# Transposes of keys, queries and last tokens moved behind attention-value products in a fused attention and expert kernel

## The chip, the cores and the metric

The kernel runs on one core of one Trainium2 chip. The time is the device time of one execution, in microseconds (us). The engines are TensorE (PE, with its weight loads as PEld), VectorE (DVE), ScalarE (ACT), GpSimd (POOL) and SyncE (SP, which here issues DMAs only).

## The reference

Attention with a relative-position bias, and behind it a mixture of experts that is routed by a hash of the token id:

```python
scores = scale * q @ k^T                    # 8 batches, 8 heads, 576 tokens, head size 64
scores = scores + bias_table[bucket(|i - j|)]    # one bias per head and distance bucket
attn = softmax(scores)
x = (attn @ v) laid out as 4608 tokens x 512
expert = token_ids * 2654435761 mod 8
out[token] = relu(x[token] @ w1[expert]) @ w2[expert]    # 512 -> 1024 -> 512
```

## The kernel before, in words

**Stages.** The attention stage runs up to about 222 us, writes each token's row with a scatter into a table in HBM that is sorted by expert, and the expert stage (line 802 on) then reads that table expert by expert. The change lies in the attention stage.

**Tiles of the attention.** Two heads make a pair; `pairs` lists 32 of them, four (m = 0 to 3) per batch b. Each pair has five groups g. Groups 0 to 3 are 128 keys each against 512 of the 576 queries; group 4 holds the rest, that is the last 64 tokens of the sequence, as queries and as keys. For a group, `products` multiplies keys and queries into one of three PSUM slots `ps`, `add_bias` adds the bias on TensorE, and `scores` has ScalarE write the exponentials to `att`. A third slot lets `add_bias` of the next group start early.

**The order.** It is written out by hand (lines 744 to 763): each engine works through its instructions in program order. A turn of the loop takes two groups and issues, on TensorE, the score products, the bias, then what `early` holds, then what `behind` holds for the first and for the second group, then the bias of the group that follows. `behind` advances a stream of attention-value (AV) products by nine per group. The stream runs one to two pairs behind the scores: pair p starts at group 2 of pair p+1. Its 45 steps are 27 for three output tiles in the PSUM bank aux0 and 18 for two in the bank aux1 (`px` in `av_steps`, line 511). At the end of each part VectorE takes a reciprocal (`rcp`, line 546) and multiplies into `x_all` (line 547), which empties the bank. As a pair has five groups, even pairs have groups 2 and 3 in one turn, odd pairs groups 3 and 4.

**What the change moves.**
- `transpose_qk` (line 370): eight TensorE transposes of the cast keys and queries of a pair into `pqk`, which has the bank aux1, and two VectorE copies to `kt` and `qt`. `early` issues it for pair n+2 at group 3 of pair n.
- `cast_rest` (line 246): two VectorE casts of the last tokens' queries and keys of the next batch (`qrh`, `krh`), in `behind` at (m, g) = (1, 3).
- `transpose_rest` (line 388): four transposes of these into `pr`, which has the bank aux0, and three VectorE copies to `kzr` and `qtr`; in `early` at (2, 0).
- `cast_vrest` (line 256): two POOL casts of the last tokens' values, in `pair_start` at m = 2, between `cast_qk` and the scatters.
- `load_rest` (line 199): eight DMAs on SP for the last tokens of a batch, in `pair_start` of the batch before (m = 0). Its tiles `qr`, `kr`, `vr` have one buffer each.

**Other work in the way.** `pair_start` also issues loads, the cast of `qh` and `kh` for three pairs ahead on POOL (two buffers each, so the cast waits for the transposes of two pairs before), and from pair 12 on two scatters per pair (`dispatch`, line 561, POOL; four in the last pairs). At pair 4 `route_load` has SP load the token ids into `te`; from pair 6 on `behind` issues one step of `route` per group, first on VectorE (`te`, `ef`, `oh`), then two ranking matmuls into `rps` (line 309).

Of the kernel before, what the change touches and what calls it, by code (L numbers as in the profile page):

```python
# [11 lines left out]
F32 = mybir.dt.float32  # L12
# [19 lines left out]
def kernel(  # L32
# [13 lines left out]
    B, H, S, D = q.shape  # L46
# [6 lines left out]
    P = 128  # L53
    NPAIR = H // 2
# [21 lines left out]
    for dl in range(3):  # L76
        for y in range(GN):
            r = 2 * y - MAXD + dl - 1
# [71 lines left out]
    with tc.tile_pool(name="at", bufs=1) as at, tc.tile_pool(  # L150
        name="atp", bufs=1, space=bass.MemoryType.PSUM
    ) as atp:

        def aux(i, shape, dtype, name):
            return atp.tile(shape, dtype, name=name, tag=f"aux{i}", bufs=1,
                            space=bass.MemoryType.PSUM)
# [24 lines left out]
        qr, kr, vr = {}, {}, {}  # L181

        def load(j, which="qkv", eng=None, h0=0, h1=4):
            for key, dst, src in (("q", qf, q), ("k", kf, k), ("v", vf, v)):
                if key not in which:
                    continue
                if j not in dst:
                    dst[j] = at.tile([P, 4, NT, 2 * D], F32, name=key + "f",
                                     bufs=3)
                for T in range(NT):  # L190
                    (eng or nc.sync).dma_start(  # L191
                        out=dst[j][:, h0:h1, T, :],
                        in_=bass.AP(
                            src.tensor, (4 * j + h0) * S * D + 2 * P * D * T,
                            [[2 * D, P], [S * D, h1 - h0], [1, 2 * D]],
                        ),
                    )

        def load_rest(b, which="qkv", eng=None):
            for key, dst, src in (("q", qr, q), ("k", kr, k)):  # L200
                if key not in which:
                    continue
                dst[b] = at.tile([P, 2, 2 * D], F32, name=key + "r", bufs=1)
                for hh in range(2):
                    (eng or nc.sync).dma_start(
                        out=dst[b][:, hh, :],
                        in_=bass.AP(
                            src.tensor, ((b * H + hh) * S + NB4) * D,
                            [[2 * D, RU], [2 * S * D, NPAIR], [1, 2 * D]],
                        ),  # L210
                    )
            if "v" in which:
                vr[b] = at.tile([P, NPAIR, D], F32, name="vr", bufs=1)
                for hh in range(2):
                    for c in range(2):
                        r0 = D * hh + RU * c
                        (eng or nc.sync).dma_start(
                            out=vr[b][r0 : r0 + RU, :, :],
                            in_=bass.AP(
                                v.tensor, ((b * H + hh) * S + NB4 + c) * D,  # L220
                                [[2 * D, RU], [2 * S * D, NPAIR], [1, D]],
                            ),
                        )
# [146 lines left out]
        def transpose_qk(n, eng=None):  # L370
            pqk = aux(1, [P, 2, KT * P], F16, "pqk")
            for i, src in enumerate((kh, qh)):
                for t in range(KT):
                    T, c = t // 2, t % 2
                    o = P * t if i == 0 else NT * P * c + P * T
                    nc.tensor.transpose(  # L376
                        out=pqk[:, i, o : o + P],
                        in_=src[n][:, t, :, :].rearrange("p h d -> p (h d)"),
                        identity=ident[:, :],
                    )  # L380
            kt = at.tile([P, KT * P], F16, name="kt", bufs=3)
            nc.vector.tensor_copy(out=kt[:, :], in_=pqk[:, 0, :])  # L382
            kts[n] = kt
            qt = at.tile([P, KT * P], F16, name="qt", bufs=3)
            nc.vector.tensor_copy(out=qt[:, :], in_=pqk[:, 1, :])
            qts[n] = qt

        def transpose_rest(b):
            pr = aux(0, [P, 2, 2, P], F16, "pr")
            for i, key in enumerate("kq"):  # L390
                for c in range(2):
                    nc.tensor.transpose(
                        out=pr[:, i, c, :],
                        in_=rh[b, key][:, c, :, :].rearrange(
                            "p h d -> p (h d)"
                        ),
                        identity=ident[:, :],
                    )
            for hh in range(2):
                nc.vector.tensor_copy(  # L400
                    out=kzr[b % 2][D * hh : D * hh + D, :,
                                   D * hh : D * hh + D].rearrange(
                        "p m (c u) -> p c m u", c=2
                    ),
                    in_=pr[D * hh : D * hh + D, 0, :, :].rearrange(
                        "p c (u m) -> p c m u", m=NPAIR
                    ),
                )
            nc.vector.tensor_copy(
                out=qtr[b % 2][:, :, :].rearrange(  # L410
                    "p m (c u) -> p c m u", c=2
                ),
                in_=pr[:, 1, :, :].rearrange(
                    "p c (u m) -> p c m u", m=NPAIR
                ),
            )
# [157 lines left out]
        def advance(it, count):  # L574
            for _ in range(count):
                if next(it, "end") == "end":
                    return
# [18 lines left out]
        nc.scalar.dma_start(out=idents[:, :, :], in_=I128_d.ap())  # L596
        load(0, "q", None, 0, 2)
        load_rest(0, "kq", nc.scalar)

        cast_qk(0, nc.vector, nc.vector)  # L600
# [63 lines left out]
        nc.sync.dma_start(out=msk[:, :], in_=MSK_d.ap())  # L664
        nc.sync.dma_start(out=cnt[:, :], in_=CNT_d.ap())
        nc.sync.dma_start(out=tok[:, :], in_=TOK_d.ap())
        load(2, "qk")

        FILLS = 10

        def fill_table(i):
            rows = NSLOT // FILLS
            nc.sync.dma_start(
                out=xperm_d.ap()[rows * i : rows * (i + 1), :].rearrange(
                    "(p r) d -> p (r d)", p=P
                ),
                in_=zx[:, :, :].rearrange("p r d -> p (r d)"),
            )

        NP = len(pairs)  # L680
# [12 lines left out]

        def pair_start(n):
            b, m = pairs[n]
            if b + 1 < B and m == 0:
                load_rest(b + 1)
            if n % 2 == 0 and n + 6 < NP:
                load(n // 2 + 3, "qk")
            if n % 2 == 0 and n + 4 < NP:  # L700
                load(n // 2 + 2, "v")
            if n == 4:
                route_load()
            if 2 <= n < 2 + FILLS:
                fill_table(n - 2)
            if n + 3 < NP:
                cast_qk(n + 3)
            if b + 1 < B and m == 2:
                cast_vrest(b + 1)
            if n >= 6 and pairs[n - 2][1] == 0:  # L710
                waiting.extend((pairs[n - 6][0], t) for t in range(NIT))
            if n >= 12:
                for _ in range(2 if n < NP - 2 else 4):
                    if waiting:
                        dispatch(*waiting.pop(0))
            if n >= 22 and n % 2 == 0 and n < 30:
                (load_w2 if n % 4 == 0 else load_w1)((n - 22) // 4)

        def behind(n, g):
            G = NIT * n + g  # L720
            b, m = pairs[n]
            if 6 <= n < 12:
                next(routing, None)
            if G >= NIT + 2:
                advance(av, 9)
            if g == 2 and n + 1 < NP:
                cast_v(n + 1)
            if (m, g) == (1, 3) and b + 1 < B:
                cast_rest(b + 1, nc.vector)

        def early(n, g):
            b, m = pairs[n]
            if (n, g) in ((0, 1), (1, 0)):
                transpose_qk(n + 1)
            if g == 3 and 0 < n < NP - 2:
                transpose_qk(n + 2)
            if (m, g) == (2, 0) and b + 1 < B:
                transpose_rest(b + 1)
            if (n, g) == (1, 0):
                rest_rest(0)  # L740
            if (m, g) == (3, 3) and b + 1 < B:
                rest_rest(b + 1)
# [25 lines left out]
    with tc.tile_pool(name="mo", bufs=1) as mo, tc.tile_pool(  # L768
        name="mop", bufs=1, space=bass.MemoryType.PSUM
# [83 lines left out]
    with tc.If(over > 0):  # L853
        with tc.tile_pool(name="fb", bufs=1) as fb, tc.tile_pool(
            name="fbp", bufs=1, space=bass.MemoryType.PSUM
# [126 lines left out]
```

## Time and profile before

| what | us |
|---|---|
| median of 3 runs | 396.09 (395.26 to 398.11) |
| the profiled execution | 397.42 |
| its span, first to last instruction | 395.6 |
| TensorE busy | 337.3 (85%) |
| ScalarE busy | 202.5 (51%) |
| GpSimd busy | 160.7 (41%) |
| VectorE busy | 133.2 (34%) |

Times in the rows are counted from the first instruction of the profiled execution. A matmul's end is modelled and matmuls overlap, so TensorE's pace is read from the starts. In brackets stands the idle time of the engine ahead of an instruction, and what ended it.

### The profile page before, as it was taken

What the parts mean: (1) busy time and instruction counts of PE and PEld (TensorE: products, weight loads), DVE (VectorE), ACT (ScalarE), POOL (GpSimd) and SP (SyncE); (2) the same over time, 40 slices, a digit from 0 to 9 for tenths busy, and PEclk for the clock granted to TensorE, in tenths of its full rate; (3) what the DMA queues carried; (4) which work ended last, traced back from release to release, by engine and by line L of the source; (5) the groups of instructions that cost most, each with busy time, mean ns of one, the idle gap of its engine ahead of it and who ended that gap; (6) DMA issues with size and microseconds to landing.
All of it is one profiled execution on the core that took longest, in us unless ns stands there. A gap on an engine that the chain in (4) does not pass through costs nothing.

```text
span 395.6 us, 9129 instructions
## 1 busy us (share of the span) xinstructions
PE 337.3 (85%) x3796; PEld 207.1 (52%) x3796; DVE 133.2 (34%) x322; ACT 202.5 (51%) x235; POOL 160.7 (41%) x229
## 2 busy tenths in 40 slices
PE   2667994999988889799998429999999999999990
PEld 1225662566555555465664316574756565665640
DVE  2204353554453433535422210405132322323120
ACT  1345881798778867788896204150504142332410
POOL 6125241142756656764743300334251515141231
PEclk9968997799999999999999958999999999999997
DMA  5998978999879487399871160799999999994221
GB/s 151 246 278 220 302 177 195 252 261 280 239 203 284 116 225 225 72 246 213 160 128 49 42 210 11 157 174 186 218 234 180 268 154 261 164 261 100 92 82 53
DMA packets 93491, 72.85 MB, mean 184 GB/s; under 512 B 14167, under 2 KB 84599, under 8 KB 93440
## 3 DMA queue, kind: packets, MB, share of 16 engines
q1 hardware_dynamic: 73616, 40.13, 37.9%
q0 software_dynamic: 17664, 30.96, 37.0%
q10 hardware_dynamic: 2160, 1.09, 1.0%
q8 instruction: 32, 0.52, 0.5%
q14 instruction: 19, 0.16, 0.1%
HBM read 69.47 MB, written 21.03 MB: 229 GB/s over the span
## 4 chain that ended last, share of the span: by engine, by line
PE 75%; DMA 8%; DVE 5%; SPq 4%; issue 2%; ACT 2%; POOL 1%; POOLq 0%; ACTq 0%; DVEq 0%
PE hps L812 18%; PE ops L830 17%; PE ps L441 11%; PE px L537 11%; PE ps L464 9%; PE pqk L376 4%; PE xps L791 3%; DVE x_all L547 2%; DMA qr<-in_q_dram 2%; SPq L191 2%; PE ps L498 2%; ACT att L506 2%; SPq L274 2%; DMA btb<-t_f 1%; DMA vf<-in_v_dram 1%
## 5 line engine op out<-in xcount | busy, mean ns | idle before, releaser
L506 ACT ACTIVATE att<-ps 128x1024 f16<-128x1024 f32 x160 | 153.4, 1026 | 53.1 <-PE ps L464 27.9
L818 ACT ACTIVATE h<-hps 128x640 f16<-128x640 f32 x64 | 45.1, 704 | 112.5 <-PE hps L812 112.2
L441 PE MATMUL ps<-btb,idents 128*128 128x384 f16 (+1 forms) x384 | 79.8, 294 | 3.5 <-DMA btb<-t_f 3.5
L812 PE MATMUL hps<-xpt,w1t 128*128 128x320 f16 x512 | 72.8, 303 | 0.0
L830 PE MATMUL ops<-w2t,h 128*128 128x512 f16 x320 | 72.7, 379 | 0.0
L838 POOL DMA_INDIRECT out_dram<-ok,xpn x40 | 39.2, 981 | 57.4 <-DVE ok L837 50.5
L812 PEld LDWEIGHTS <-w1t 128*128 128x128 f16 x512 | 50.8, 99 | 21.4
L537 PEld LDWEIGHTS <-att 128*128 128x128 f16 x1408 | 56.6, 99 | 7.2 <-issue 1.4
L537 PE MATMUL px<-va,att 128*128 128x65 f16 x1280 | 58.1, 195 | 0.9 <-issue 0.4
L830 PEld LDWEIGHTS <-h 128*128 128x128 f16 x320 | 30.7, 98 | 33.5
L562 POOL DMA_INDIRECT t_xperm<-x_all,ds x40 | 39.5, 987 | 19.0 <-DVE rcp L546 9.5
L464 PE MATMUL ps<-qt,kt 64*128 64x512 f16 x256 | 45.1, 401 | 1.5 <-ACT att L506 0.8
L441 PEld LDWEIGHTS <-idents 128*128 128x128 f16 x464 | 29.0, 99 | 30.9 <-issue 29.5
L837 DVE COPY ok<-ops 128x512 f32<-128x512 f32 x40 | 27.7, 692 | 46.9 <-PE ops L830 46.9
L795 DVE COPY xpt<-xps 128x640 f16<-128x640 f16 x32 | 15.0, 489 | 74.4 <-PE xps L791 73.4
L229 POOL CAST qh<-qf 128x512 f16<-128x512 f32 x31 | 19.1, 617 | 45.6 <-PE pqk L376 33.0
L237 POOL CAST va<-vf 128x512 f16<-128x512 f32 x32 | 19.8, 619 | 40.3 <-PE px L537 30.3
L546 DVE RECIPROCAL rcp<-px 128x6 f32<-128x6 f32 x64 | 11.9, 186 | 61.6 <-PE px L537 47.3
L547 DVE TENSOR_TENSOR x_all<-px,rcp 128x384 f16<-128x384 f32 x64 | 31.4, 491 | 2.2
L382 DVE COPY kt<-pqk 128x512 f16<-128x512 f16 x32 | 13.6, 425 | 51.4 <-PE pqk L376 49.2
L464 PEld LDWEIGHTS <-kt 64*128 64x128 f16 x512 | 14.0, 95 | 30.9 <-issue 27.8
L133 POOL DMA_DIRECT2D w1t<-in_moe_w_dram x8 | 6.5, 816 | 52.1 <-PE xps L791 52.1
(71 smaller groups left out, 243.8 us busy)
## 6 DMA issues: line engine op xcount, KB each, us to landing
w1t<-in_moe_w_dram POOLq DMA_DIRECT2D x8, 1024.0 KB
w2t<-in_moe_w_dram POOLq DMA_DIRECT2D x8, 1024.0 KB
qf<-in_q_dram SPq DMA_DIRECT2D x30, 256.0 KB
kf<-in_k_dram SPq DMA_DIRECT2D x30, 256.0 KB
vf<-in_v_dram SPq DMA_DIRECT2D x30, 256.0 KB
t_xperm<-zx SPq DMA_DIRECT2D x10, 514.0 KB
xpn<-t_xperm SPq DMA_DIRECT2D x8, 642.5 KB
vr<-in_v_dram SPq DMA_DIRECT2D x32, 32.0 KB
```

The source lines that it names most:

```text
L237: nc.gpsimd.tensor_copy(out=va[n % 3][:, :, :D], in_=vf[n // 2][:, 2 * (n % 2) : 2 * (n % 2) + 2].rearrange("p h t (c d) -> p (h t c) d", ...
L441: nc.tensor.matmul(out=out, lhsT=idents[:, which, :], rhs=rhs, start=start, stop=True, skip_group_check=True,)
L464: nc.tensor.matmul(out=ps[:, hh, o : o + rhs.shape[1]], lhsT=lhsT, rhs=rhs, start=not biased and (g < KT or t == 0), stop=True, skip_group ...
L506: nc.scalar.activation(out=att[:, g, :, :], in_=ps[:, :, :], func=AF.Exp, bias=0.0, scale=scale,)
L537: nc.tensor.matmul(out=po, lhsT=lhsT, rhs=rhs, start=(i == 0), stop=(i == len(todo) - 1), skip_group_check=True,)
L547: nc.vector.tensor_tensor(out=x_all[:, b, its[0] : its[0] + ni, :DM].rearrange("p t (m h d) -> p t m h d", h=2, m=NPAIR)[:, :, m, :, :], i ...
L562: sc_in = nc.gpsimd.indirect_dma_start(out=xperm_d.ap()[:, :], out_offset=bass.IndirectOffsetOnAxis(ap=ds2[:, B * t + b : B * t + b + 1], ...
L812: nc.tensor.matmul(out=hps[:, nr, :NR], lhsT=w1h[:, kt, ts(ft, P)], rhs=xt[e][:, kt, ts(nr, NR)], start=(kt == 0), stop=(kt == NPT - 1),)
L818: nc.scalar.activation(out=h1[:, ft, :].rearrange("p (r n) -> p r n", r=NRC), in_=hps[:, :, :NR], func=AF.Relu, bias=0.0, scale=1.0,)
L830: nc.tensor.matmul(out=ops[:, :], lhsT=h1[:, ft, ts(kc, P)], rhs=w2h[:, ft, :], start=(ft == 0), stop=(ft == NFT - 1),)
L837: nc.vector.tensor_copy(out=ok[:, :], in_=ops[:, :])
L838: so = nc.gpsimd.indirect_dma_start(out=out[:, :], out_offset=bass.IndirectOffsetOnAxis(ap=xn[e][:, kc, DM:XW].bitcast(I32), axis=0), in_= ...
```

## The change

`transpose_qk` at group 3 moves from `early` to `behind`, after the nine AV products of that group. `transpose_rest` moves there too, and from (2, 0) to (3, 0). `cast_rest` moves from (1, 3) to (2, 2), `cast_vrest` from m = 2 to m = 3. The last tokens' tiles get two buffers. The last tokens of batch 1 are loaded in the setup, ahead of the keys and queries of pairs 4 and 5, and no longer at pair 0.

```diff
-                dst[b] = at.tile([P, 2, 2 * D], F32, name=key + "r", bufs=1)
+                dst[b] = at.tile([P, 2, 2 * D], F32, name=key + "r", bufs=2)
...
-                vr[b] = at.tile([P, NPAIR, D], F32, name="vr", bufs=1)
+                vr[b] = at.tile([P, NPAIR, D], F32, name="vr", bufs=2)
...
         nc.sync.dma_start(out=tok[:, :], in_=TOK_d.ap())
+        load_rest(1)
         load(2, "qk")
...
-            if b + 1 < B and m == 0:
+            if 0 < b < B - 1 and m == 0:
                 load_rest(b + 1)
...
-            if b + 1 < B and m == 2:
+            if b + 1 < B and m == 3:
                 cast_vrest(b + 1)
...
             if G >= NIT + 2:
                 advance(av, 9)
+            if g == 3 and 0 < n < NP - 2:
+                transpose_qk(n + 2)
+            if (m, g) == (3, 0) and b + 1 < B:
+                transpose_rest(b + 1)
             if g == 2 and n + 1 < NP:
                 cast_v(n + 1)
-            if (m, g) == (1, 3) and b + 1 < B:
+            if (m, g) == (2, 2) and b + 1 < B:
                 cast_rest(b + 1, nc.vector)
 
         def early(n, g):
             b, m = pairs[n]
             if (n, g) in ((0, 1), (1, 0)):
                 transpose_qk(n + 1)
-            if g == 3 and 0 < n < NP - 2:
-                transpose_qk(n + 2)
-            if (m, g) == (2, 0) and b + 1 < B:
-                transpose_rest(b + 1)
             if (n, g) == (1, 0):
                 rest_rest(0)
```

## Rows read from the trace of the kernel before

**Rows 1.** Waits of TensorE: us in total, times, longest us.
```profile
PE pqk L376 <- DVE x_all L547: 8.5, 6, 4.3
PE pr L392 <- DVE x_all L547: 6.3, 7, 2.1
PE ps L464 <- ACT att L506: 2.4, 6, 0.8
```

**Rows 2.** Busy time by stretch: PE, PEld, DVE, ACT, POOL, PEclk, DMA, GB/s.
```profile
85.50:108.70 23.20, 22.08 (x354) 13.65 (x353) 10.85 (x30) 18.93 (x21) 12.21 (x19) 1.00 0.94 244
108.70:206.00 97.30, 88.10 (x1417) 55.36 (x1417) 42.81 (x117) 78.84 (x87) 60.38 (x86) 1.00 0.79 188
```

**Rows 3.** Timeline (start us, us, instructions) around one batch's last tokens.
```profile
87.83 0.75 DVE L249 CAST qrh<-qr 128x256 f16<-128x256 f32 x1
88.50 0.48 DVE L249 CAST krh<-kr 128x256 f16<-128x256 f32 x1
...
89.11 0.56 DVE L547 TENSOR_TENSOR x_all<-px,rcp 128x384 f16<-128x384 f32 x1
...
89.73 0.28 PE L392 MATMUL pr<-idents,krh 128*128 128x128 f16 x2 [0.69 <-DVE x_all L547]
```

**Rows 4.** Timeline around three pairs of scatters.
```profile
125.51 0.97 POOL L562 DMA_INDIRECT t_xperm<-x_all,ds  x1 [0.30 <-issue]
...
127.03 0.18 DVE L546 RECIPROCAL rcp<-px 128x4 f32<-128x4 f32 x1 [2.53 <-PE ps L441]
...
127.82 0.38 PE L376 MATMUL pqk<-idents,kh 128*128 128x128 f16 x4 [0.96 <-DVE x_all L547]
...
128.26 0.71 PE L537 MATMUL px<-va,att 128*128 128x65 f16 x18
...
131.16 0.97 POOL L562 DMA_INDIRECT t_xperm<-x_all,ds  x1 [0.30 <-issue]
...
132.67 5.62 ACT L506 ACTIVATE att<-ps 128x1024 f16<-128x1024 f32 x6 [1.10 <-PE px L537]
...
134.37 0.39 PE L376 MATMUL pqk<-idents,kh 128*128 128x128 f16 x4
...
138.72 0.97 POOL L562 DMA_INDIRECT t_xperm<-x_all,ds  x1 [0.30 <-issue]
...
141.01 0.38 PE L376 MATMUL pqk<-idents,kh 128*128 128x128 f16 x4 [1.14 <-DVE x_all L547]
```

**Rows 5.** Timeline around the first routing steps.
```profile
55.28 6.73 SPq L274 DMA_DIRECT2D te<-in_moe_token_ids_dram  x6
...
63.85 0.18 DVE L286 TENSOR_SCALAR te<-te 128x40 int32<-128x40 int32 x1 [3.78 <-DMA te<-in_moe_token_ids_dram]
...
64.97 0.59 PE L376 MATMUL pqk<-idents,kh 128*128 128x128 f16 x4 [4.34 <-DVE x_all L547]
...
66.69 0.87 DVE L299 TENSOR_TENSOR oh<-ef,msk 128x320 f16<-128x320 f32 x1
...
67.71 0.43 PE L309 MATMUL rps<-oh,cnt 128*128 128x320 f16 x1 [1.24 <-DVE oh L299]
...
70.02 1.02 ACT L506 ACTIVATE att<-ps 128x1024 f16<-128x1024 f32 x1 [8.06 <-PE ps L464]
```

**Rows 6.** Busy time of two stretches with a lower granted clock (columns as in rows 2).
```profile
30.00:40.00 10.00, 7.88 (x106) 5.14 (x102) 4.79 (x13) 5.74 (x6) 5.54 (x10) 0.83 0.81 221
60.00:75.00 15.00, 9.43 (x98) 5.75 (x96) 5.41 (x17) 5.47 (x6) 1.60 (x3) 0.66 0.96 251
```

**Rows 7.** Timeline of a turn with groups 4 and 0.
```profile
83.08 0.43 PE L537 MATMUL px<-va,att 128*128 128x65 f16 x9
83.36 0.49 PE L441 MATMUL ps<-btb,idents 128*128 128x384 f16 x2
83.52 0.56 DVE L547 TENSOR_TENSOR x_all<-px,rcp 128x384 f16<-128x384 f32 x1
```

**Rows 8.** Timeline of SP's queue around the early loads.
```profile
25.41 0.98 SPq L191 DMA_DIRECT2D qf<-in_q_dram  x2
...
33.05 0.98 SPq L191 DMA_DIRECT2D qf<-in_q_dram  x2
```

## The prediction

> **What bounds the kernel now.** I read the times first, then the waits of TensorE, the busy time by stretch, and last the timeline around the waits. The profiled execution took 397.42 us, 1.33 us over the median 396.09 (span 395.6). All sums are made against 397.42, and the 1.33 is taken off at the end. The change touches the attention stage alone, up to about 222 us; the expert stage behind it stays as it is.
>
> In the list of TensorE's waits the reader is to see that ScalarE holds TensorE for 2.4 us only, while the two transposes of this change wait for VectorE's `x_all` multiply: 8.5 us for `pqk` in 6 waits and 6.3 us for `pr` in 7 [rows 1]. The multiply empties the PSUM bank (aux1 for `pqk`, aux0 for `pr`) that the transposes want. In the windows, one batch of four pairs takes 23.2 us from 85.5 on. Once token scatters run twice per pair, the 97.3 us from 108.7 to 206 hold four batches, 24.3 us each: TensorE is idle for 97.3 - 88.1 = 9.2 us of them and ScalarE for 18.5 [rows 2]. So TensorE bounds the stage, with ScalarE close behind.
>
> The timeline shows three causes.
> - Last tokens: the casts `qrh` (0.75) and `krh` (0.48), 1.23 us together, stand on VectorE ahead of the reciprocal and the multiply at 89.11, and `pr` starts at 89.73 after 0.69 us of idle time [rows 3].
> - Scatters: TensorE goes on issuing, but what waits for it is released late, about 1.5 us after the start of the second scatter of a pair: scatter 125.51, reciprocal 127.03; 131.16 and ACT 132.67. I counted eleven such pairs between 106 and 193 us; two are shown. The `pqk` transposes then wait for the late multiply, 0.96 us at 127.82 and 1.14 at 141.01 [rows 4].
> - The token ids: SP issues the `te` loads in the 6.73 us from 55.28, VectorE's first routing step starts at 63.85, and everything behind it on VectorE, so also `pqk`, waits, 4.34 us. ScalarE stands still for 8.06 us until 70.02 [rows 5]. The granted clock of 60 to 75 us is 0.66, which is 10.2 us at half (1.2 GHz) and the rest at full (2.4 GHz); from 30 to 40 us it is 0.83, 3.4 us at half [rows 6].
>
> **Part 1: `transpose_qk` behind the products.** No instruction is added: eight transposes take 128.26 - 127.82 = 0.44 us in either place [rows 4]. For an even pair, (n,2) and (n,3) share a loop turn, so they now stand behind eighteen AV products (0.71 us with the tail, about 0.5 of issue); for an odd pair behind nine (0.28 us from 83.08 to the next work of TensorE at 83.36) [rows 4, 7]. AV products of that turn write aux0, which is free, so the even pairs' waits, 0.96 and 1.14 us in the rows, lose 0.5 us. But the casts of the next `qh` and `kh` on POOL wait for the transposes (both tiles have two buffers), and the scatters stand behind these casts on POOL. The scatters so start 0.28 us later behind an odd pair, and the release with them. Net 0.5 - 0.28, between 0.2 and 0.3, taken as 0.28, for each of five waits (the list has six, one of them the 4.34 of the token ids [rows 1, 5]): 5 x 0.28 = 1.4 us gained. Bounds: 5 x 0.5 = 2.5 gained, and 0 if the release moves as far as the transposes.
> `kt` and `qt` are needed two pairs later, and aux1 is wanted again only by the second nine AV products of the next turn, over 1.2 us behind; the two copies fit. If the casts of part 3 (1.23 us, once in a batch) stand in front of them, one copy's worth of waiting, some 0.4 us as at 66.69 behind 64.97, is lost in each of seven batches: 2.8 at most. I take 0, because these casts wait for no transposes and start before them.
>
> **Part 2: `cast_vrest` a pair later.** On POOL it stands between the casts and the scatters. From the transposes to the second scatter it takes 131.16 - 127.82 = 3.34 us without it and 138.72 - 134.37 = 4.35 with it [rows 4]. So 1.0 us leaves the chain from pair m = 1 to the even pair m = 2, which is two loop turns long and is set by the late release: 4 batches x 1.0 = 4.0 us. It comes back between m = 2 and m = 3, which is three turns long (134.37 - 127.82 = 6.55 us in the rows), where TensorE is not held by the release of the transposes' bank. Bounds: 0 (it only moves) and 4.0; I take 4.0, since the late multiply is what ends last at 141.01, behind the scatter with the long chain [rows 4].
>
> **Part 3: last tokens, cast at (2,2), transposed at (3,0).** The 1.23 us of casts leave the reciprocal's way. But at (3,0) the transposes follow only nine products after the last product of aux0: the multiply that empties it ends at 83.52 + 0.56 = 84.08 in such a turn, while TensorE is through with these nine at 83.36 [rows 7]. So `pr` waits 0.72 us there against 0.69 now: the wait does not go, its cause is a new one. In the two batches without scatters that is 0. In the four with scatters the old wait lay beside the late release and the new one lies in the longer interval: between 0 and 4 x 0.72 = 2.9 us lost; I take half, 1.4, as ScalarE is the one that waits there for part of the time (18.5 us idle against 9.2 for TensorE) [rows 2].
>
> **Part 4: the loads.** `load_rest(1)` goes ahead of `load(2, "qk")`. SP issues the same twelve loads between 25.41 and 33.05 in another order, and from there on in the old one [rows 8]. The q and k of pairs 4 and 5 land up to 5 us later, so pair 4's transposes may wait at about 36 us; the 2.1 us wait for the first last tokens, the longest of `pr` [rows 1], goes. None of this counts, because the `te` loads come at SP's own time and VectorE stands ready 3.78 us before they land [rows 5]: 3.78 us of delay are free there, and any gain before it is lost. The second buffers of `qr`, `kr`, `vr` take away waits of SP's loads; SP is ahead of need later on, so 0.
> At the `te` wait itself the order behind it changes. Now `pqk` runs first and its two copies stand ahead of `oh` (66.69), so the ranking matmul starts at 67.71. After the change `oh` follows the multiply that `pqk` waits for at 64.97 directly, so at about 64.85, ends 0.87 later at 65.72, and the matmul starts at 65.75. From it to ACT's restart were 70.02 - 67.71 = 2.31 us; the eight transposes, 0.80 at the low clock (64.97 to 65.77), come on top: 68.9, a gain of 1.1. The last tokens of batch 2, until now ahead of this stall, come behind it: 0.7 lost. With the 1.24 us of idle time ahead of the matmul gone, I count 0.6 for a clock that rises sooner: if a third of the 10.2 us at half clock goes, TensorE wins back half of 3.4 us, 1.7; if none goes, 0 [rows 5, 6]. Together 1.0; bounds -0.7 and 2.1.
> The Trainium skill speaks against this 0.6. Its page "TensorE: Matmul & The Clock Gate", section "Part 4: PE-mode transpose", says that transposes do not count as work for the clock the way other matmuls do; no row here can show it. By it the clock rises no sooner and the sum is 0.6 us smaller.
>
> **Sum.** 1.4 + 4.0 - 1.4 + 1.0 = 5.0. 397.42 - 5.0 = 392.4 for the profiled kind, less 1.33: 391.1 us. The lower bounds give 0 - 2.8 + 0 - 2.9 - 0.7 = -6.4 (402.5), the upper 2.5 + 4.0 + 2.1 = 8.6 (387.5).
>
> **The rivals.**
> - *The early gain is kept.* If SP itself comes sooner to the `te` loads, the 2.1 us and the half clock behind it (3.4 us at half, 1.7) count [rows 1, 6]: 391.1 - 3.8 = 387.3. Against it: SP's loads follow each other with hardly a gap from 25.41 to the end of the `te` issues at 62.0 [rows 5, 8]. Chance 0.12.
> - *The scatters follow the transposes.* Each release moves as far as the transposes, parts 1 to 3 cancel, and only part 4 is left: 396.1 - 1.0 = 395.1. For it: the fixed 1.5 us of the releases [rows 4]. Against it: the 1.0 us of `cast_vrest`. Chance 0.23.
> - *The later casts hold the scatters.* At (2,2) the 1.23 us of VectorE casts fall on the second scatter of the pair (transposes + 3.34 us). If the scatter waits for them, four batches give back 4.9 us: 396.0. For it: `qrh` took 0.75 us beside POOL's casts [rows 3]. The Trainium skill, page "SBUF — State Buffer", section "Who interferes with whom", has such a rule: a VectorE cast can hold the port that GpSimd needs, and the loser stands still. No row shows a scatter lengthened so. Chance 0.06.
> - *The new wait falls into the late release (slower).* At (3,0) `pr` waits for the reciprocal and multiply of products that ended 0.28 us before. If that end falls into the 1.5 us behind a second scatter, the wait is not 0.72 but up to 2.2 us. Five batches x 1.5 = 7.5: 391.1 + 7.5 = 398.6, and 402.6 with the 4.0 of part 2 lost as well. The point from which it decides: the second scatter must start within some 2 us of the transposes of m = 2; by the 4.35 us of part 2 [rows 4] it starts later, so I think it misses. Chance 0.09.
>
> **How the numbers follow.** The forecast has 0.50, with a range of its own from 388.5 to 394. A measurement of this kernel tells about 1% (4 us) from no change. Under 392.1 lie six tenths of the forecast and the first rival, with a little of the others: 0.46. Over 400.1 lies a part of the last: 0.06. The rest, 0.48, is within 1%. The range runs from 386.5, the first rival and a little more of the upper bounds, to 398, short of the last rival and of the lower bounds together: under 0.2 is left out.
>
> **What would show it.** Right: `pqk` no longer waits for `x_all` by 0.7 us and more at even pairs; the four batches from 108.7 on take about 23.3 us each; `pr` still waits some 0.7 us, at the head of pair m = 3; `te` still starts near 63.8 us, with VectorE waiting longer for it than 3.78. Wrong: `te` two or more us sooner, `pr` waiting 1.5 us and more, or batches still at 24.3 us.

## The result and the profile after

The changed kernel takes 393.13 us (median of 9 runs, 391.44 to 396.04); the kernel before took 398.0 us in the same series (9 runs, 395.26 to 400.17). The ratio is 0.9888 (95% interval 0.9847 to 0.9928): 4.9 us less, where 5.0 were forecast (391.1 us, worked out from a kernel before at 396.09). The kernel before takes from 385 to 399 us, by the chip, so each ratio below is one to the kernel before on the same chip.

The page of the changed kernel, its first lines:

```profile
span 390.9 us, 9127 instructions
...
PE 334.0 (85%) x3796; PEld 207.9 (53%) x3796; DVE 130.1 (33%) x322; ACT 202.7 (52%) x235; POOL 159.8 (41%) x229
```

The span is 4.7 us shorter than the 395.6 before, and TensorE's busy time 3.3 us; TensorE still bounds the kernel with 85%. To see where, I take two marks that both kernels have: the key transposes of pair 12, some 8 us ahead of the first scatter (100.21 before, 101.42 after), and those of pair 28, four batches later. The timeline of the kernel before, these two lines:

```profile
92.15 0.38 PE L376 MATMUL pqk<-idents,kh 128*128 128x128 f16 x4
...
189.33 0.38 PE L376 MATMUL pqk<-idents,kh 128*128 128x128 f16 x4 [0.43 <-PE ps L441]
```

The same lines of the changed kernel:

```profile
91.75 0.39 PE L376 MATMUL pqk<-idents,kh 128*128 128x128 f16 x4
...
183.75 0.38 PE L376 MATMUL pqk<-idents,kh 128*128 128x128 f16 x4
```

Up to pair 12 the change gains 0.4 us. The four batches behind it take 183.75 - 91.75 = 92.0 us instead of 97.2, that is 23.0 each: 5.2 us gained. From there to the end of the span it takes 0.9 us longer (207.15 against 206.27). So the whole gain is in the stretch with two scatters per pair.

The waits of TensorE after the change (us in total, times, longest), the four lines that matter here:

```profile
PE pqk L376 <- POOL kh L229: 6.7, 2, 3.8
PE rps L309 <- DMA t_xperm<-zx: 5.7, 1, 5.7
...
PE pr L392 <- DVE x_all L547: 3.1, 6, 0.6
...
PE pqk L376 <- DVE x_all L547: 0.6, 2, 0.4
```

The `pqk` transposes' wait for the multiply was 8.5 us [rows 1] and is 0.6. `pr` still waits for it, six times and never over 0.6 us (0.72 was forecast). Two entries have grown: `pqk` waits 6.7 us for the cast `kh` (4.0 before), a matter of the early loads, and `rps` waits 5.7 (1.2 before), which is the stall of the token ids in another place: TensorE now stands still at the ranking matmul and no longer at `pqk`. The list names a DMA that fills the table as its cause, but the matmul starts 0.15 us behind the end of `oh`, which it reads (67.08 + 0.48 against 67.71 in the rows of part 4 below).

### The profile page after: what moved, and what is told of

Its sections match the earlier page's. It is cut to its first block, busy times and chain, and to the rows that moved or that the text cites. A ratio compares the mean times of both kernels' runs of the same rounds, so it can differ in the third digit from the quotient of the medians.

```text
span 390.9 us, 9127 instructions
## 1 busy us (share of the span) xinstructions
PE 334.0 (85%) x3796; PEld 207.9 (53%) x3796; DVE 130.1 (33%) x322; ACT 202.7 (52%) x235; POOL 159.8 (41%) x229
## 4 chain that ended last, share of the span: by engine, by line
PE 76%; DMA 7%; SPq 6%; DVE 4%; issue 2%; ACT 1%; POOL 1%; POOLq 0%; ACTq 0%; DVEq 0%
PE hps L813 18%; PE ops L831 18%; PE ps L441 12%; PE px L537 10%; PE ps L464 9%; PE pqk L376 3%; SPq L191 3%; PE xps L792 3%; SPq L274 2%; DMA btb<-t_f 2%; DVE x_all L547 2%; PE ps L498 2%; ACT att L506 1%; DMA kf<-in_k_dram 1%; DMA xpn<-t_xperm 1%
## 5 line engine op out<-in xcount | busy, mean ns | idle before, releaser
L506 ACT ACTIVATE att<-ps 128x1024 f16<-128x1024 f32 x160 | 153.4, 1025 | 47.3 <-PE ps L464 26.8
L537 PEld LDWEIGHTS <-att 128*128 128x128 f16 x1408 | 58.2, 98 | 12.2 <-DVE qt L385 2.9
L537 PE MATMUL px<-va,att 128*128 128x65 f16 x1280 | 59.8, 194 | 2.5 <-DVE qt L385 2.0
L464 PE MATMUL ps<-qt,kt 64*128 64x512 f16 x256 | 43.5, 395 | 1.3 <-ACT att L506 1.0
```

The costliest lines, as they stand in the source:

```text
L464: nc.tensor.matmul(out=ps[:, hh, o : o + rhs.shape[1]], lhsT=lhsT, rhs=rhs, start=not biased and (g < KT or t == 0), stop=True, skip_group ...
L506: nc.scalar.activation(out=att[:, g, :, :], in_=ps[:, :, :], func=AF.Exp, bias=0.0, scale=scale,)
L537: nc.tensor.matmul(out=po, lhsT=lhsT, rhs=rhs, start=(i == 0), stop=(i == len(todo) - 1), skip_group_check=True,)
```

## The experiments

Twelve kernels were run, on three chips: e1, e2, e3 and e9 on the first (kernel before: 385.28 us, 35 runs), e5 to e8 on the second (396.82, 11 runs), e10 to e13 on the third (398.99, 7 runs). On the first chip the kernel before is 12 to 14 us faster, for a reason that turned out to be the heart of the case. The kernel before was traced, and the changed kernel run, in the series of the result alone, and the record does not name its chip: what is set against these two below stands against another series.

One table is worked out from all the traces: the mean interval, over the four batches from pair 12 to pair 28, from the transposes issued at one pair to those issued at the next, in us (m is the place in its batch of the pair at which they are issued). It shows which part of a batch an edit shortens.

| kernel | m0 to m1 | m1 to m2 | m2 to m3 | m3 to m0 | four batches |
|---|---|---|---|---|---|
| before | 6.43 | 6.22 | 6.46 | 5.18 | 97.2 |
| after | 5.98 | 4.72 | 7.29 | 5.01 | 92.0 |
| e12, part 1 alone | 6.01 | 6.45 | 6.66 | 4.68 | 95.2 |
| e13, all but part 2 | 6.37 | 4.52 | 7.31 | 4.69 | 91.6 |
| e5, before without scatters | 6.03 | 5.64 | 6.03 | 4.48 | 88.7 |
| e6, after without scatters | 5.76 | 4.53 | 7.01 | 4.53 | 87.3 |
| e1, part 1 alone (first chip) | 5.76 | 5.99 | 5.98 | 4.53 | 89.1 |
| e9, part 2 alone (first chip) | 6.03 | 5.44 | 6.03 | 4.48 | 87.9 |
| e2, all but part 2 (first chip) | 5.76 | 4.53 | 7.02 | 4.53 | 87.3 |
| e3, all but part 3 (first chip) | 5.76 | 5.68 | 5.98 | 4.53 | 87.8 |
| e10, after, scatters apart | 5.76 | 4.61 | 7.02 | 4.52 | 87.7 |

### The parts one by one, on the first chip

Part 1 alone, on the kernel before:

```diff
@@ behind
                 advance(av, 9)
+            if g == 3 and 0 < n < NP - 2:
+                transpose_qk(n + 2)
@@ early
-            if g == 3 and 0 < n < NP - 2:
-                transpose_qk(n + 2)
```

> The kernel before with one edit: transpose_qk of pair n+2 at group 3 stands behind the nine products. Theory A (each part has its own share, as in the prediction): 1.4 us faster than before, ratio about 0.996; the wait of pqk for x_all falls from 8.5 us to about 5, the interval between the transposes of m = 1 and m = 2 stays near 6.6 us, pr still waits 0.69 us six times. Theory B (the move of these transposes is the whole change, since their waits sum to 4.2 us beside the one at the token ids): 4 to 5 us faster, ratio 0.988 to 0.990, m = 1 to m = 2 near 5 us.

Measured: 382.79 us, ratio 0.9926 (0.9896 to 0.9955).

Part 2 alone, on the kernel before (with the second buffer of `vr` that it needs):

```diff
-                vr[b] = at.tile([P, NPAIR, D], F32, name="vr", bufs=1)
+                vr[b] = at.tile([P, NPAIR, D], F32, name="vr", bufs=2)
...
-            if b + 1 < B and m == 2:
+            if b + 1 < B and m == 3:
                 cast_vrest(b + 1)
```

> The kernel before with one edit: the POOL casts of the last tokens' values (cast_vrest) stand at m = 3, with two buffers for vr. Theory A: 4.0 us faster, ratio about 0.990; in the four batches with scatters the transposes of m = 2 follow those of m = 1 after some 5.6 us in place of 6.6, and m = 3 follows m = 2 after the 6.5 us that it took. Theory B: no difference, within 1 us. Theory C (the casts only move, the delay comes back between m = 2 and m = 3): no difference in the sum, m = 1 to m = 2 at 5.6 and m = 2 to m = 3 at 7.5 us.

Measured: 383.88 us, ratio 0.997 (0.9949 to 0.9992).

The change without part 2:

```diff
-            if b + 1 < B and m == 3:
+            if b + 1 < B and m == 2:
                 cast_vrest(b + 1)
```

> The kernel after the change with cast_vrest back at m = 2. Theory A: the 4.0 us go, about 397 us where the kernel after takes 393, ratio to before about 0.998; m = 1 to m = 2 at about 6 us in place of 4.9. Theory B and C: as the kernel after, ratio about 0.989.

Measured: 384.75 us, ratio 0.9984 (0.9959 to 1.001).

The change without part 3:

```diff
@@ behind
-            if (m, g) == (3, 0) and b + 1 < B:
-                transpose_rest(b + 1)
...
-            if (m, g) == (2, 2) and b + 1 < B:
+            if (m, g) == (1, 3) and b + 1 < B:
                 cast_rest(b + 1, nc.vector)
@@ early
+            if (m, g) == (2, 0) and b + 1 < B:
+                transpose_rest(b + 1)
```

> The kernel after the change with the last tokens' casts back at (1,3) and their transposes back in early at (2,0). Theory A: the wait of pr moves back to the short interval; by the prediction's term 1.4 us faster than the kernel after, ratio to before 0.985, pr waits 0.7 us, m = 2 to m = 3 shorter by 0.7 to 0.9 us and m = 1 to m = 2 longer by less than that. Rival D (the 1.23 us of casts on VectorE ahead of reciprocal and multiply are what holds TensorE): 2 to 4 us slower than the kernel after, ratio 0.995 to 1.0, pr waiting 1 us and more.

Measured: 382.62 us, ratio 0.9922 (0.9894 to 0.995).

None of the mechanisms that counted on late releases came true, because on this chip there are none. (For e2 Theory A's ratio of 0.998 came out, but by chance: it had m1 to m2 at about 6 us, and it is 4.53.) The timeline of e9 around a pair of scatters (start, us; in brackets the idle time before, and what ended it):

```profile
131.94 1.05 POOL L562 DMA_INDIRECT t_xperm<-x_all,ds  x1
...
133.29 0.97 POOL L562 DMA_INDIRECT t_xperm<-x_all,ds  x1 [0.31 <-issue]
...
134.54 0.17 DVE L546 RECIPROCAL rcp<-px 128x4 f32<-128x4 f32 x1
134.57 1.94 ACT L506 ACTIVATE att<-ps 128x1024 f16<-128x1024 f32 x2 [0.78 <-PE ps L464]
...
135.31 0.38 PE L376 MATMUL pqk<-idents,kh 128*128 128x128 f16 x4
```

The two scatters stand 1.35 us apart, and 1.29 in the kernel before (124.22 and 125.51), but the reciprocal at 134.54 has no idle time ahead of it and the transposes at 135.31 none either. In all four traces of this chip no reciprocal from 85 to 200 us starts more than 0.04 us behind both the end of its products and VectorE's work before it; in the kernel before twelve start 0.28 to 1.46 us behind. The intervals of e9 in the table repeat to 0.01 us from batch to batch. So this chip shows what the edits do where no scatter holds anything. There, part 3 takes 1.15 us out of m1 to m2 (e3 5.68, e6 4.53, which differ in part 3, in the scatters and in the chip, and neither has a late release) and puts 1.03 into m2 to m3 (5.98 to 7.01). Part 2 takes 0.2 out of m1 to m2: three of the four intervals of e1 are 5.88 to 5.89 (the first, 6.32, raises its mean), and e3 has 5.68; from e5 to e9 it is 5.64 to 5.44. Beside part 3 it adds nothing: e2 lacks it and has 4.53 like e6. Both parts relieve the same interval, and part 3 by itself is enough.

It also shows the start of the kernel, on one chip and without disturbance: pair 12's transposes come at 89.06 in e1, 91.34 in e9, 91.77 in e2 and 89.76 in e3. So part 1 alone comes there 2.3 us before part 2 alone; with the last tokens moved and `cast_vrest` not (e2), pair 12 is 2.0 us later than the other way about (e3), and what e3 has more than e1, the loads above all, costs 0.7.

### The scatters left out, on the second chip

35 of the 40 scatters (the token rows of batches 0 to 6) are taken from the list and not issued, in the kernel before (e5) and the changed one (e6), so these rows are missing from the expert stage's input.

```diff
                     if waiting:
-                        dispatch(*waiting.pop(0))
+                        waiting.pop(0)
```

> The kernel before without the scatters of batches 0 to 6 (35 of 40 left out, so their tokens never reach the expert table). If the late releases come from the scatters (theory S): between pairs 12 and 24 the waits of pqk for x_all go but for the one at the token ids, the time from the transposes of pair 12 to those of pair 28, 96.9 us, falls by 6 to 9 us to about 89, and a batch takes 22.3 us. If they come from elsewhere, from POOL's casts or from VectorE's own queue (rival Q): 1 us less at most, 96 us.

> The kernel after the change, without the same 35 scatters. By theory S nearly all that the change gains between pairs 12 and 28 (96.9 to 92.0 us) is gained at the scatters, so without them the two kernels differ by 1 us or less in this stretch: about 88 to 89 us, and the whole gain of the change falls from 4.9 to 1 or 2 us. By rival Q the difference of 4.9 us stays.

Measured: e5 384.15 us, ratio 0.9655 (0.96 to 0.971); e6 383.05 us, ratio 0.9615 (0.9554 to 0.9677). The windows from pair 12 to pair 28 (us, then busy us of PE, PEld, DVE, ACT and POOL, the clock, the DMA share and GB/s), e5:

```profile
92.50:181.20 88.70, 85.44 (x1400) 54.41 (x1400) 42.46 (x116) 77.64 (x85) 34.34 (x59) 1.00 0.80 193
```

The same of e6:

```profile
90.60:177.90 87.30, 84.86 (x1406) 55.27 (x1403) 39.80 (x116) 77.42 (x85) 33.98 (x59) 1.00 0.82 202
```

And the kernel before with its scatters, for comparison:

```profile
92.10:189.30 97.20, 87.68 (x1400) 54.53 (x1401) 42.73 (x116) 76.70 (x85) 60.22 (x85) 1.00 0.79 206
```

The kernel before falls by 12.7 us, to the level of the first chip, and the change is then worth 1.1 us (384.15 to 383.05) instead of 4.9; the 1.1 lies within the noise of four runs each. In the kernel before TensorE is busy for 87.7 of the 97.2 us and without scatters for 85.4 of the 88.7: of the 8.5 us that go, 6.2 are waiting. No reciprocal is late in e5 or e6. So some 3.8 of the 4.9 us are won at the late releases that the forecast read from [rows 4]. In this stretch alone the scatters cost 97.2 - 88.7 = 8.5 us before and 92.0 - 87.3 = 4.7 after.

### Routing from pair 8, on the second chip

The steps of `route` start two pairs later, so that VectorE no longer stands at the token ids; on the kernel before (e7) and the changed one (e8).

```diff
-            if 6 <= n < 12:
+            if 8 <= n < 12:
                 next(routing, None)
```

> The kernel before with the routing steps from pair 8 on in place of pair 6. Theory T (VectorE's wait for the token ids holds everything at 60 to 70 us): te waits 0, the 4.34 us of pqk go and the clock does not fall there, 5 to 8 us faster, ratio 0.980 to 0.987. Rival U (the loads hold that stretch anyway): the wait comes back as a wait of casts for loads, 2 us or less.

> The kernel after the change with the routing steps from pair 8 on. Theory T: 5 to 8 us faster than the kernel after, ratio to before 0.968 to 0.977. The prediction says that what is gained or lost ahead of the token ids is swallowed there; with the wait gone it shows: the start to pair 8 was 1 us later in the kernel after (81.5 against 80.5 us at the transposes of pair 10 in its terms), so if that is from the order of the loads the distance to the kernel before with the same edit shrinks from 4.9 to 3 or 4 us, and if it was chance it stays.

Measured: e7 391.09 us, ratio 0.9798 (0.9739 to 0.9858); e8 385.57 us, ratio 0.9721 (0.9673 to 0.9769). The stall is gone; the timeline of e8 at the first routing step:

```profile
70.02 3.77 ACT L506 ACTIVATE att<-ps 128x1024 f16<-128x1024 f32 x4 [0.41 <-PE ps L464]
...
70.33 0.38 DVE L286 TENSOR_SCALAR te<-te 128x40 int32<-128x40 int32 x1
...
73.11 0.39 PE L376 MATMUL pqk<-idents,kh 128*128 128x128 f16 x4
```

ScalarE stands still for 0.41 us here, the routing step and the transposes not at all, and the windows of e8 show the full clock:

```profile
60.00:75.00 15.00, 14.39 (x240) 9.49 (x237) 8.94 (x25) 12.71 (x15) 6.30 (x14) 1.00 0.93 248
```

The same window read 9.43 us of TensorE at a clock of 0.66 before [rows 6]. Without the stall the change is worth 5.5 us (391.09 to 385.57), no less than with it, and again in the stretch from pair 12 to pair 28 (98.1 us in e7, 92.6 in e8): the gain does not come from the order behind the token ids.

### The scatters set apart, on the third chip

If a release is late because two scatters follow each other at once, one scatter at the head of the pair and one in its middle should cost nothing. e10 is the change with this; e11 has the later routing as well.

```diff
-                for _ in range(2 if n < NP - 2 else 4):
+                for _ in range(1 if n < NP - 2 else 4):
...
                 cast_v(n + 1)
+            if g == 2 and 12 <= n < NP - 2 and waiting:
+                dispatch(*waiting.pop(0))
```

> The kernel after the change with the two scatters of a pair apart: one at the head of the pair, one behind the cast of the values at group 2 (pairs 12 to 29). Theory P (it is the second scatter right behind the first that makes releases late): where the kernel before loses time at scatters (about 397 us), no release comes later than usual, the transposes of pairs 12 to 28 span 88 us in place of 92, and the kernel takes 388 to 389 us, ratio about 0.98. Theory E (each scatter makes releases late on its own): twice as many, shorter delays, 91 to 93 us between the same transposes and a ratio near 0.988. Where the kernel before takes about 385 us, no scatter delays anything and it is as the kernel after.

> The kernel after the change with both edits: the scatters of a pair apart, and the routing steps from pair 8 on. If the two gains add up (theory P and the 7 us that the later routing gave): 380 to 383 us where the kernel before takes 397, ratio 0.958 to 0.965; where it takes 385, ratio 0.975 to 0.985 from the routing alone. Theory E: 385 us, ratio 0.972.

Measured: e10 388.38 us, ratio 0.9736 (0.9667 to 0.9804); e11 380.63 us, ratio 0.9565 (0.9492 to 0.9638). The timeline of e10:

```profile
130.75 3.77 ACT L506 ACTIVATE att<-ps 128x1024 f16<-128x1024 f32 x4 [0.27 <-PE ps L464]
...
131.11 0.98 POOL L562 DMA_INDIRECT t_xperm<-x_all,ds  x1 [0.15 <-issue]
...
131.68 0.22 PE L537 MATMUL px<-vt,rr 128*128 128x130 f16 x1
...
132.50 0.18 DVE L546 RECIPROCAL rcp<-px 128x4 f32<-128x4 f32 x1 [1.36 <-PE px L537]
...
133.26 0.98 POOL L562 DMA_INDIRECT t_xperm<-x_all,ds  x1 [0.16 <-PE ps L441]
...
133.57 0.39 PE L376 MATMUL pqk<-idents,kh 128*128 128x128 f16 x4
```

The scatters stand 2.15 us apart, with other work of POOL between them, ACT goes on after 0.27 us, and the transposes do not wait. The four batches take 87.7 us, the same as without scatters (87.3), on a chip where two at a time are late (e12 and e13 below).

That is Theory P's time, but not its mechanism, for a lone scatter holds a release as well. The products end at 131.68 + 0.22 = 131.90, and the reciprocal comes at 132.50, 0.60 us later and 1.39 us behind the start of the scatter. Five reciprocals of e10 up to 144 us come so, 1.34 to 1.39 us behind a lone scatter and 0.5 to 0.7 us behind their products. On the first chip the same place looks otherwise, in e2:

```profile
122.78 0.98 POOL L562 DMA_INDIRECT t_xperm<-x_all,ds  x1 [0.17 <-DVE x_all L547]
...
123.25 0.22 PE L537 MATMUL px<-vt,rr 128*128 128x130 f16 x1
...
123.51 0.18 DVE L546 RECIPROCAL rcp<-px 128x4 f32<-128x4 f32 x1 [0.79 <-PE px L537]
```

There the products end at 123.47, 0.69 us behind the start of the scatter, and the reciprocal follows 0.04 us later. So Theory E had the delays, one for a scatter and shorter, and was wrong on their cost: they are over before the transposes want the bank. What e10 shows is that it is enough here to set the scatters apart. As one of the two also moves to another place in the pair, it does not tell the distance from the place. e11 is the fastest version that was run.

### Parts 1 and 3 again, on the third chip

The first chip could not price the parts where releases are late, so e12 is e1 again and e13 is e2 again.

> The kernel before with only transpose_qk behind the products, as in the first such run, where no release was late behind scatters and it gained 2.8 us, all of it ahead of pair 10. Where the kernel before takes about 397 us: by the prediction's first part 1.4 us of gain between the transposes of pairs 12 and 28 (97.2 us before), so about 96 us there; if the whole gain at the scatters hangs on the order of transposes and products, 92 to 93 us. Outside that stretch the 2 to 3 us of the first run come on top: 392 to 394 us.

> The kernel after the change with cast_vrest back at m = 2, as in the first such run, where no release was late and its place made no difference. Where the kernel before takes about 397 us: by the prediction's second part the 4 us return, 96 us between the transposes of pairs 12 and 28, m = 1 to m = 2 near 6 us and 397 us in all; if the casts only move the delay, 92 us and 393 us.

Measured: e12 392.55 us, ratio 0.9875 (0.9807 to 0.9942); e13 389.43 us, ratio 0.9766 (0.9703 to 0.9829). The timeline of e12 from the transposes of m = 1 to those of m = 2:

```profile
129.82 0.39 PE L376 MATMUL pqk<-idents,kh 128*128 128x128 f16 x4
...
131.80 0.48 DVE L249 CAST krh<-kr 128x256 f16<-128x256 f32 x1
...
133.03 0.28 PE L392 MATMUL pr<-idents,krh 128*128 128x128 f16 x2 [0.96 <-DVE x_all L547]
...
133.26 0.65 PE L537 MATMUL px<-va,att 128*128 128x65 f16 x16
...
134.16 0.97 POOL L562 DMA_INDIRECT t_xperm<-x_all,ds  x1 [0.30 <-issue]
...
135.68 0.18 DVE L546 RECIPROCAL rcp<-px 128x4 f32<-128x4 f32 x1 [0.92 <-PE ps L441]
...
136.47 0.38 PE L376 MATMUL pqk<-idents,kh 128*128 128x128 f16 x4 [0.60 <-DVE x_all L547]
```

The casts (`qrh` from 131.14 on, then `krh`) push the multiply, `pr` waits for it, and the AV products of aux1 start only at 133.26, 3.44 us behind the transposes. The reciprocal that closes them falls behind the second scatter (134.16) and comes 1.52 us after its start, at 135.68. The same stretch of e13:

```profile
134.14 0.39 PE L376 MATMUL pqk<-idents,kh 128*128 128x128 f16 x4
...
136.23 0.65 PE L537 MATMUL px<-va,att 128*128 128x65 f16 x16
...
137.03 0.18 DVE L546 RECIPROCAL rcp<-px 128x4 f32<-128x4 f32 x1 [0.79 <-PE px L537]
...
137.14 0.98 POOL L562 DMA_INDIRECT t_xperm<-x_all,ds  x1 [0.28 <-POOL vt L259]
...
137.78 0.45 DVE L249 CAST krh<-kr 128x256 f16<-128x256 f32 x1
...
138.43 0.98 POOL L562 DMA_INDIRECT t_xperm<-x_all,ds  x1 [0.30 <-DVE krh L249]
...
138.66 0.39 PE L376 MATMUL pqk<-idents,kh 128*128 128x128 f16 x4
...
141.41 0.99 POOL L562 DMA_INDIRECT t_xperm<-x_all,ds  x1
...
141.96 0.29 PE L392 MATMUL pr<-idents,krh 128*128 128x128 f16 x2 [0.61 <-DVE x_all L547]
```

With the casts and `pr` gone from here the products start 2.09 us behind the transposes, 1.35 sooner, and the reciprocal at 137.03 stands ahead of both scatters. Nothing is late at this place, and the interval is 4.52 us, although `cast_vrest` still stands on POOL ahead of the scatters. For comparison the changed kernel itself, where `cast_vrest` is gone from this place too:

```profile
133.07 0.39 PE L376 MATMUL pqk<-idents,kh 128*128 128x128 f16 x4
...
135.14 0.99 POOL L562 DMA_INDIRECT t_xperm<-x_all,ds  x1 [0.15 <-issue]
...
135.71 0.22 PE L537 MATMUL px<-vt,rr 128*128 128x130 f16 x1
...
136.43 0.97 POOL L562 DMA_INDIRECT t_xperm<-x_all,ds  x1 [0.30 <-issue]
...
137.18 0.18 DVE L546 RECIPROCAL rcp<-px 128x4 f32<-128x4 f32 x1 [2.01 <-PE ps L464]
...
137.97 0.38 PE L376 MATMUL pqk<-idents,kh 128*128 128x128 f16 x4 [0.21 <-PE ps L441]
```

The scatters now come 1 us sooner, as the forecast said of part 2, but that is the wrong direction: they catch the reciprocal again. Its products end at 135.71 + 0.22 = 135.93; it starts at 137.18, 1.25 us later, where in e13 it followed its products at once. The interval is 4.90 instead of 4.52. It is a small loss, and of the other three batches (4.53, 4.92, 4.53) one has it.

The times themselves: e12 came out as expected (392 to 394 us; 95.2 us in the stretch), and it has the whole change's gain by itself, with a ratio of 0.9875 beside 0.9888. e13 lies below both of its expectations (397 and 393 us) and is 3.1 us faster than e12 on one chip. The whole change was not run in this series, so its distance to e13 is open.

## Why the prediction was right in total, and where its parts were wrong

The total was right: 5.0 us forecast, 4.9 measured, and the place was right too, 23.0 us a batch against some 23.3. The terms were not, and that their sum fits is luck.

**Part 2, forecast +4.0, is the step that failed.** It said that `cast_vrest` lengthens the chain to the second scatter by 1.0 us, and that the late release moves with it. Take it back (e13) and the four batches take 91.6 us against 92.0 in the changed kernel: it is worth nothing there, rather -0.4 by two profiles of different series, and m1 to m2 stays short. The error lies in reading the late multiply of [rows 4] as fixed to the scatter. What decides is on which side of the scatters the products end: if their reciprocal gets through first, a later scatter costs nothing and even helps. Whether part 2 would be worth something without part 3, on a chip with late releases, was not tried.

**Part 3, forecast -1.4, had the wrong sign.** I saw that 1.23 us of casts leave the reciprocal's way and that the `pr` wait only changes its place, and priced the new place. I did not follow the old one on: 1.35 us sooner for the products of aux1 is what takes their reciprocal ahead of the scatters. From e12 to e13 the four batches fall by 95.2 - 91.6 = 3.6 us, 4 x (6.45 - 4.52) = 7.7 from m1 to m2, less 4 x (7.31 - 6.66) = 2.6 at the new place and 1.5 in the other two intervals. The loads of part 4 lie between these two kernels as well, but in this stretch they differ in the second buffers alone. Without late releases part 3 only moves some 1.1 us from one interval to the next (e3, e6). Ahead of the stretch it costs: on the first chip pair 12 comes 2.0 us later in e2 than in e3, though e3 has part 2 besides. Part 3 on its own was not run on a chip with late releases, so its 3.6 is a difference of two single profiles; the timelines show the mechanism.

**Part 1, forecast +1.4,** was of the right size in the stretch: 97.2 - 95.2 = 2.0 in e12. The even pairs' waits, 8.5 - 4.3 = 4.2 us without the one at the token ids, are 1.8 in e12, a fall of 2.4 where 5 x 0.5 was said; the 0.6 of the changed kernel comes with the other parts. But the forecast had none of its gain ahead of the stretch: pair 12's transposes come at 88.80 in e12, 3.35 us sooner than before (92.15). In all e12 is 6.4 us under the kernel before on its chip, and e1 2.5 on the chip without late releases.

**The sum in the stretch.** 1.4 + 4.0 - 1.4 = 4.0 was forecast; 2.0 + 3.6 - 0.4 = 5.2 was measured. Two wrong terms, 4.4 too high and 5.0 too low, cancel. The 3.6 and the -0.4 carry what was said above of single profiles.

**Part 4, forecast +1.0.** At pair 12 the change is 0.4 us ahead, from two terms that were both mis-sized: a restart behind the token ids that is worth more, but comes with part 1, and `te` itself, which comes later. By themselves the moved loads cost time, 0.7 to 1.0 us by the traces below. The timeline of the changed kernel at the token ids, to be held against [rows 5]:

```profile
57.48 6.86 SPq L274 DMA_DIRECT2D te<-in_moe_token_ids_dram  x6
...
65.95 0.18 DVE L286 TENSOR_SCALAR te<-te 128x40 int32<-128x40 int32 x1 [6.28 <-DMA te<-in_moe_token_ids_dram]
...
67.08 0.48 DVE L299 TENSOR_TENSOR oh<-ef,msk 128x320 f16<-128x320 f32 x1
...
67.71 0.43 PE L309 MATMUL rps<-oh,cnt 128*128 128x320 f16 x1 [5.71 <-DMA t_xperm<-zx]
...
73.04 0.28 PE L392 MATMUL pr<-idents,krh 128*128 128x128 f16 x2 [0.61 <-DVE flag L329]
```

The order is the forecast one: from `te` to `oh` 1.13 us instead of 2.84, and to the ranking matmul 1.76 instead of 3.86. VectorE waits longer for `te`, 6.28 us against 3.78, and the last tokens come behind the stall, at 73.04, all as said. The clock rises sooner as well:

```profile
60.00:75.00 15.00, 8.68 (x111) 5.48 (x108) 6.07 (x19) 5.97 (x7) 2.63 (x6) 0.77 0.92 210
```

At a mean of 0.77, 2 x 0.23 x 15 = 6.9 us are at half (1.2 GHz) and the rest at full (2.4 GHz), against 10.2 before: the third that I had counted. From `te` to pair 12 it is now 91.75 - 65.95 = 25.8 us instead of 28.3, so this term is 2.5 in the two profiles. In the other kernels that route from pair 6 it is 25.5 to 26.3 where part 1 is in (seven kernels), and 26.8 and 27.6 where it is not (e9, e5): it goes with part 1, and the three kernels without part 1 differ by 1.5 among themselves. The 0.7 that I counted for the last tokens behind the stall may be seen in e2 (26.3) against e3 (25.5).

The other term ate most of it: `te` did not stay near 63.8 but came at 65.95. The forecast held SP's queue to be fixed because the loads follow each other without gaps. 1.16 of the 2.1 us stand already ahead of the moved loads, since SP comes to them at 26.57 and not at 25.41 [rows 8], behind loads that are the same in both kernels. Over all traces the first routing step comes at 63.2 to 65.0 with the old order (five kernels, mean 64.0) and at 63.8 to 66.0 with the new (six, mean 65.0), so the reorder costs about 1.0, and two runs of one order differ by as much. On the first chip, e3 against e1, it is 0.7 at pair 12. The early wait that part 4 accepted is there too:

```profile
39.19 0.40 PE L376 MATMUL pqk<-idents,kh 128*128 128x128 f16 x4 [2.87 <-POOL kh L229]
```

Pair 4's keys are late, as said ("at about 36 us"), and the stall behind the token ids does hide it.

**The clock.** The 10.2 us at half fell to 6.9 with eight transposes in that restart, as the sum had it. But the same window has 0.77 in e9 as well, where the transposes stand as in the kernel before, and 0.89 (3.3 us at half) in e1, e3 and e12, so the third that was counted does not hang on the place of these transposes alone. The Trainium skill, page "TensorE: Matmul & The Clock Gate", section "Part 4: PE-mode transpose", says that a transpose does not count as a busy TensorE in the same way; this case does not decide on it: other matmuls stand in the restart too, and no run of this case tests transposes by themselves.

**The rivals.** *The early gain is kept*: no, `te` came later rather than sooner. *The scatters follow the transposes*, and only part 4 is left: no; it needs 24.3 us a batch, and it is 23.0. *The later casts hold the scatters*: no; in e13 the casts `qrh` and `krh` lie beside the first of two scatters (`krh` at 137.78), and both scatters take 0.98 us, as before (0.97 in [rows 4]). *The new wait falls into the late release*: no; none of the six `pr` waits is over 0.6. The margin is small, though: in e13 `pr` at 141.96 starts 0.55 us behind a first scatter.

## What to carry to other kernels

A wait that ends on a late event is removed by getting through ahead of that event, not by moving the event; look for the edit that crosses it, and price a moved operation at the place it leaves as carefully as at the place it comes to. Where an engine issues two indirect scatters straight behind each other, try them apart before tuning anything around them: here the change with that and with a later start of what waits for a slow load is 4.35% under the kernel before (e11), the change alone 1.1%, each against the kernel before in its own series. And price the parts of a change one by one even when the total fits; here it fitted by two errors of 4 to 5 us of opposite sign, and one part of the four, run alone in another series, has the gain of the whole (0.9875 and 0.9888 of the kernel before).

## What the runs showed of the hardware that was not expected

The same scatters hold releases on one chip and not on another. Of the three chips of the experiments one, with the kernel before at 385.28 us, shows no late release in four traces; on the others the kernel before takes 396.82 and 398.99, and leaving out 35 scatters brings it to 384.15 on one of them. Each chip was used at one time only, so chip and time are not told apart. Nor is it a fixed 1.5 us behind the second scatter, as the forecast read it: it is 1.52 in e12 and 0.75 in the changed kernel (136.43 to 137.18). And it does not take two: behind a lone scatter of e10 the reciprocal comes 1.34 to 1.39 us after the scatter's start, with its products done 0.5 to 0.7 us before. Not every release beside a scatter is held, though: in e10 products that end at 149.22, 0.19 us behind a scatter's start, are followed by their reciprocal at 149.26, and in e11, with its scatters placed alike on the same chip, none up to 199 us is over 0.2 us late. Which ones are held, and why scatters hold releases on two chips and not on the third, is not settled by these runs.
